# Feed-forward groups of 3, 4, 4 and 5 weight tiles, and conversion steps of two tiles interleaved

## The chip, the cores and the metric

The kernel runs on one core of a Trainium2 chip. The metric is the device time of one execution in microseconds, as the median of several runs. A profile is of one execution, and its times are counted from the start of its span. Engines are named as the profile names them: PE multiplies matrices, PEld is its weight load, DVE, ACT and POOL work on tiles element by element, SP issues transfers.

## The reference

Three parts follow one another; each takes the output of the one before.

```python
# attention over hashed buckets: 2 x 8 heads, 768 positions, 64 wide
mask = q_bucket[:, :, :, None] == k_bucket[:, :, None, :]
scores = np.where(mask, scale * q @ k.T, -1e9)
attn = exp(scores - scores.max(-1)); attn /= attn.sum(-1) + 1e-9
x = (attn @ v) laid out as 1536 tokens x 512
# first feed-forward part, w_in 512 x 2048, w_out 2048 x 512 (float64 in memory)
h = x @ w_in
x = where(h > 0, h, exp(min(h, 0)) - 1) @ w_out
# second part: 4 experts, each relu(x @ w1[e]) @ w2[e], weighted by normalized probabilities
```

## The kernel before

**Numbers.** Every matrix product is made of three PE products of two-part numbers (high part and rest), so each operand is split into a high and a low tile. The weights of the first feed-forward part are 64-bit in memory. [...]

**Weight tiles.** The hidden width 2048 is cut into 16 weight tiles of 128 columns of `w_in` and the matching 128 rows of `w_out`. A tile takes 18 steps, each taken from a list one at a time, most of them one instruction over half the tile (128x512): two on ACT (L243), then on DVE two each of L244, L245, L247, L249 and L250, then two additions L257 (on POOL, or on DVE if `adder` says so), one step that frees the raw buffer and lets SP issue the next load (`consumed`, L202), two splits (each ACT L274, then DVE L278; the first for the `w_in` half, the second for the `w_out` half), and one more that only keeps the books. There are three raw buffers, so a load goes out three tiles ahead.

**Groups.** Before the change there are four groups of four tiles. For each group the kernel goes through three blocks of 512 tokens, and for each block through the tiles of the group: 48 pairs (group, block, tile) in the list `seq` (L793). A pair has a first product l1 (L709 to L711, 12 matmuls) whose result goes through ACT L738 and L739, DVE L742, ACT L743 and POOL L747 to become `h`, and a second product l2 (L763, 12 matmuls) from `h`. After the last tile of a block the four PSUM tiles are added to the sum in SBUF (`epilogue`, L776: a copy by ACT L780 in the first group, DVE L782 after that).

**Order of the work.** The order is written out by hand, and each engine takes its instructions in the order in which they are issued. In step n of the main loop (L1203) the kernel issues l1 of pair n and its L738 and L739, then l2 of pair n-2 and its epilogue, then L742, L743 and L747 of pair n, and then some conversion steps (L837: nine a step in the first twelve steps, then six). Eight weight tiles have room in SBUF, and the dictionary `todo` (L795) says from which step on each is converted. The tiles are converted one after the other: all 18 steps of one, then those of the next.

**Ends of attention.** Three weight tiles (0, 1 and 2) are converted during attention (L674 to L681). The letters of `TAIL` (L75) order the last attention steps together with l1 of pairs 0 to 3 (`p`, `o`, `q`), l2 of pairs 0 to 2 (`k`), and conversion steps (`f`, 35 of them, with the additions on DVE; `s` runs what is missing of tile 3 and splits it). `c`, `n`, `g` finish the last attention output, which l1 needs for its last 128 input rows. In the ends of attention L747 is on DVE (`GL` is 0). Pair 1 uses a PSUM tile that l2 of pair 0 needs next.

Tiles are numbered t0 to t15 below, in the order of use.

Of the kernel before, what the change touches and what calls it, by code (L numbers as in the profile page):

```python
# [16 lines left out]
P = 128  # L17
# [18 lines left out]
def lsh_attention_moe_kernel(  # L36
# [14 lines left out]
    nc = tc.nc  # L51
# [3 lines left out]
    DFF = w_in.shape[1]  # L55
# [8 lines left out]
    TB = 512  # L64
    NTB = NT // TB
    GM = 8
    GP = 4
    G1 = DFF // (P * GP)
    NG = G1 + E
    NPRE = 2  # L70
    WA = 3
    ORDER = "CETHQtNLhlMmdV"
    WARM = (9, 2, 5)
    GL = 0.0
    TAIL = "AfffffffoqfpBpcpprffofffffpfpqppVfVfffVfncxkgfffgfozqfsfkffppffppoffqffk"  # L75

    mm = nc.tensor.matmul

# [104 lines left out]


    wide = w_in.dtype != F32
    wraw, w32, wt = {}, {}, {}

    raw_free, raw_used = [raw_p], []
    ld_n = [0]
    keep = {}  # L190
    ld_list = [(g, m) for g in range(NG) for m in range(0, GP if g < G1 else GM, 1 if wide and g < G1 else 2)]

    def loads():
        while ld_n[0] < len(ld_list) and raw_free:
# [7 lines left out]
    def consumed(g, m, split):  # L202
        if (not split) if wide and g < G1 else (split and m % 2):
            raw_free.append(raw_used.pop(0))
            loads()

    def load_w(g, m):
        if g < G1:
            a, b_, f0 = w_in, w_out, (g * GP + m) * P
        else:  # L210
            a, b_, f0 = w1[g - G1], w2[g - G1], m * P
        e = 1
        if wide and g < G1:
            a, b_, e = a.bitcast(I32), b_.bitcast(I32), 2
        n = 3 - e
        t = raw_free.pop(0).tile([P, 4 * DM], I32 if e == 2 else F32, tag="raw", name="raw")
        t1 = t[:, 0:2 * DM].rearrange("p (c f) -> p c f", c=NC)
        t2 = t[:, 2 * DM:4 * DM]
        nc.sync.dma_start(out=t1, in_=a[:, f0 * e:f0 * e + 2 * P].rearrange("(c p) f -> p c f", p=P))
        nc.sync.dma_start(out=t2.rearrange("p (m d) -> p m d", m=n),  # L220
                          in_=b_[f0:f0 + n * P, :].rearrange("(m p) d -> p m d", p=P))
        for i in range(n):
            wraw[g, m + i] = (t, t1, t2, i)
# [36 lines left out]
    def split_w(g, m, pool, eng, part=None):  # L260
        if part != 1:
            wt[g, m] = pool.tile([P, 4, DM], F32R, tag="w", name="w")
        t = wt[g, m]
        for i, s in enumerate(w32[g, m]):
            if part == 1 - i:
                continue
            hi, lo = t[:, 2 * i, :], t[:, 2 * i + 1, :]
            if i == 0:
                hi = hi.rearrange("p (c f) -> p c f", f=P)
                lo = lo.rearrange("p (c f) -> p c f", f=P)  # L270
            if "p" in eng:
                nc.gpsimd.tensor_scalar(out=hi, in0=s, scalar1=1.0, scalar2=1.0, op0=ALU.mult, op1=ALU.mult)
            else:
                nc.scalar.activation(out=hi, in_=s, func=ACTF.Copy)  # L274
            if "P" in eng:
                nc.gpsimd.tensor_tensor(out=lo, in0=s, in1=hi.bitcast(F32), op=ALU.subtract)
            else:
                nc.vector.tensor_tensor(out=lo, in0=s, in1=hi.bitcast(F32), op=ALU.subtract)  # L278
        if part != 0:
            del w32[g, m]  # L280
# [470 lines left out]
    def emit_l2(g, tb, ms):  # L751
        if ms[0] == 0:
            l2_t[g, tb] = [pools["ps2" if i < 2 else "ps3"].tile([P, 512], F32, tag=f"l2_{i}", name=f"l2_{i}")
                           for i in range(4)]
        parts = [(m, wt[g, m], *h_t.pop((g, tb, m))) for m in ms]
        for i in range(4):
            ps = l2_t[g, tb][i]
            r = slice(i * P, (i + 1) * P)
            for m, w, hh, hl in parts:
                w2h, w2l = w[:, 2, :], w[:, 3, :]  # L760
                ops = ((w2h[:, r], hh), (w2h[:, r], hl), (w2l[:, r], hh))
                for n, (a, b_) in enumerate(ops):
                    mm(ps, a, b_, start=(m == 0 and n == 0), stop=(m == GP - 1 and n == 2))  # L763
            if ms[-1] == GP - 1:
                epilogue(g, tb, i, ps)

    def acc_tile(tb):
# [20 lines left out]
    def wpool(m):  # L788
        return wa_p if m < NPRE else pools["wb" if m > NPRE else "wm"]

    LAG = 2
    due = []
    seq = [(g, tb, m) for g in range(G1) for tb in range(NTB) for m in range(GP)]  # L793

    todo = {GP * NTB * (g - 1) + max(3 * m, GP + 1 + m if g == 1 else 0): (g, m) for g in range(1, G1) for m in range(GP)}  # L795

    todo2 = {4: 0, 5: 1, 6: 2, 7: 3, 10: 4, 11: 5}
    conv = []

    def l1_step(n):  # L800
# [13 lines left out]
            f()  # L814
        del fill[:n]

    def slot_of(g, m):
        return wpool((g * GP + m) % GM)

    def l2_step(n, rest=None):  # L820
        if n < LAG:
            return
        rest = rest or []
        g, tb, m = seq[n - LAG]
        emit_l2(g, tb, range(m, m + 1))
        take(rest, 1)
        if g + 1 == G1 and tb * GP + m in todo2:
            prep2(todo2[tb * GP + m])
        due.extend([todo[n]] if n in todo else [])
        if due and not conv:  # L830
            g, m = due.pop(0)
            if (g, m) not in w32:
                conv.extend(conv_w(g, m, pools["w32"], 2))
                conv.append(lambda: consumed(g, m, False))
            conv.extend(lambda i=i: split_w(g, m, slot_of(g, m), "a", i) for i in range(2))
            conv.append(lambda: consumed(g, m, True))
        take(conv, 9 if n < GP * NTB else 6)  # L837

# [91 lines left out]
    def prep2(m):  # L932
        if m == 0:
            keep["cv"] = cv_p.tile([P, 2 * DM], F32, tag="w32", name="tmp")
            keep["tmp"] = keep["cv"][:, 0:DM].rearrange("p (k d) -> p k d", k=2)
            emit_pt()
        if m < 2:
            prep_w1(0, m)
        elif m < 6:
            prep_w2(0, m - 2)  # L940
# [166 lines left out]
            unit(v, a, hooks)  # L1107


    parts, outs, fill = [], [], []  # L1110
    at = {nm: 0 for nm in "VLkq"}
    at.update(s=NPRE + 1, f=NPRE + 1)

    def l1_start(m):
        ps, pa = l1_parts(*seq[m])
# [3 lines left out]
    def step(nm):  # L1119

        if nm in "AB":
            att_step(NU - 2 + "AB".index(nm))
        elif nm == "V":
            att_step(NU + at["V"])
        elif nm == "c":
            while done:
                emit_comb(done.pop())
        elif nm == "r":
            emit_rinv(NPAIR - 1)
            emit_rx(NPAIR - 1)  # L1130
        elif nm == "n":
            for half in range(2):
                ps = ps_t.tile([P, 512], F32, tag=f"pt{2 + half}", name="r")
                emit_norm(NPAIR - 1, half, ps)
                fin.append(lambda half=half, ps=ps: emit_fin(NPAIR - 1, half, ps[:, 0:HS]))
        elif nm == "g":
            fin.pop(0)()
        elif nm == "x":
            ps_late.close()
            open_pool("ps3", 1, None, PSUM)  # L1140
            open_pool("ring", 1, None, PSUM)
        elif nm == "z":
            late.close()
            open_pool("wb", GM - NPRE - 1)
            open_pool("near", 1)
            open_pool("accp", 1)
        elif nm == "p":
            if not parts:
                at["L"] += 1
                l1_start(at["L"])  # L1150
            take(parts, 1)
        elif nm == "o":
            m, ps = outs.pop(0)
            outq.extend(l1_out(*seq[m], ps, GL))
            take(outq, 1)
        elif nm == "q":
            take(outq, 1)
        elif nm == "k":
            l2_step(at["k"] + LAG)
        elif nm == "f":  # L1160
            if not fill:
                g, m = divmod(at["f"], GP)
                fill.extend(conv_w(g, m, pools["w32"], 2, nc.vector) + [lambda: consumed(g, m, False)])
                at["f"] += 1
            take(fill, 1)
        elif nm == "s":
            m = at["s"]
            while at["f"] <= m or at["f"] == m + 1 and fill:
                step("f")
            split_w(0, m, wpool(m), "a")  # L1170
            consumed(0, m, True)
        if nm in "Vks":
            at[nm] += 1

    fin, outq = [], []
# [19 lines left out]
    for nm in TAIL:  # L1195
        step(nm)
    assert not (parts or outs or outq or fin or done)
    conv.extend(fill)
    ahead = seq[GP:]
    ahead += [(G1 + gg, tb, m) for gg in range(2 * E) for tb in range(NTB) for m in range(4)]  # L1200
    for f in l1_step(GP):
        f()
    for n in range(GP + 1, len(seq) + LAG):  # L1203
        if ahead[0][0] == G1 and "hf" not in pools:
            open2()
        rest = l1_step(n)
        if n >= len(seq):
            l1_step(n)
        l2_step(n, rest)
# [32 lines left out]
```

## Time and profile before

| | |
|---|---|
| median of 3 runs | 1058.06 us |
| lowest and highest | 1055.71 and 1058.21 us |
| the profiled execution: its own time | 1054.75 us |
| its span | 1053.0 us |
| PE busy in the span | 1019.5 us (97%) |
| DVE, ACT, POOL busy | 826.4, 520.4, 499.3 us |
| attention, roughly | 0 to 262 us |
| first feed-forward part, main run | 262 to 546 us |
| second part | 546 to 1053 us |

PE counts as busy from a matmul's start to its modelled end, and neighbours overlap: the start-to-start distance says more than the busy time. A row of a timeline gives the start, the time, the engine, the line, the tile written and read, and in brackets how long the engine had been idle and what ended that.

### The profile page before, as it was taken

The page shows a single profiled execution, that of the slowest core. Times are in us where ns is not written, and L with a number is a line of the kernel's source. Part 1 is how long each engine was busy: PE and PEld are TensorE (multiplying, and loading weights), DVE is VectorE, ACT ScalarE, POOL GpSimd, SP SyncE. Part 2 cuts the span into 40 slices and gives each one's busy share as a digit, 9 for nine tenths or more (in the row PEclk, how much of TensorE's full clock was granted, in tenths as well). Part 3 has the DMA queues.
Part 4 walks back from the last instruction along what each step waited for, and adds up shares of the span by engine and source line. Part 5 has one row for each costly group of instructions (what it writes and reads, how often), then busy time and mean ns, then how long its engine had stood idle before and what let it go on. Part 6 is the DMA issues. An engine that isn't in the chain of part 4 may idle for free.

```text
span 1053.0 us, 16050 instructions
## 1 busy us (share of the span) xinstructions
PE 1019.5 (97%) x5886; PEld 890.4 (85%) x5886; DVE 826.4 (78%) x1295; ACT 520.4 (49%) x1024; POOL 499.3 (47%) x422
## 2 busy tenths in 40 slices
PE   8999999999899999998999999999999999999996
PEld 5898998888688887886788989898898989988896
DVE  6889889889656756673658778889898888989885
ACT  6898998897455443434533324233332333233322
POOL 3466776665225343432231243545555445464464
PEclk9999999999899999999999999999999999999999
DMA  7866676561212121210020020020200102010012
GB/s 182 156 143 147 144 173 144 126 185 41 80 41 80 41 81 40 80 41 1 21 90 2 1 99 13 1 81 5 96 11 26 56 11 91 11 66 16 2 50 71
DMA packets 72694, 72.24 MB, mean 69 GB/s; under 512 B 26132, under 2 KB 60648, under 8 KB 72616
## 3 DMA queue, kind: packets, MB, share of 16 engines
q1 hardware_dynamic: 72312, 71.14, 24.6%
q8 instruction: 47, 0.77, 0.3%
q14 instruction: 31, 0.25, 0.1%
q10 hardware_dynamic: 304, 0.07, 0.0%
HBM read 48.98 MB, written 3.21 MB: 50 GB/s over the span
## 4 chain that ended last, share of the span: by engine, by line
PE 34%; DVE 7%; POOL 6%; issue 5%; ACT 1%; POOLq 0%
PE l L1006 14%; POOL a L1022 4%; PE a L955 3%; PE a L954 3%; PE a L953 3%; PE l L763 2%; PE r L955 2%; PE r L954 2%; PE r L953 2%; DVE w L895 2%; DVE temps L982 1%; POOL hf L988 1%; POOL w L895 1%; DVE temps L984 1%; ACT op L891 1%
## 5 line engine op out<-in xcount | busy, mean ns | idle before, releaser
L1006 PEld LDWEIGHTS l<-w,op 128*128 128x128 f32 x2016 | 252.1, 188 | 13.6 <-ACT op L891 5.6
L1006 PE MATMUL l<-w,op 128*128 128x256 f32 x2016 | 255.7, 281 | 3.8 <-ACT op L891 3.8
L1022 POOL TENSOR_TENSOR a<-a,temps 128x512 f32<-128x512 f32 x84 | 124.3, 1502 | 60.1 <-DVE a L1017 60.1
L747 POOL TENSOR_TENSOR h<-g,h 128x512 fp32r<-128x512 f32 x44 | 62.9, 1430 | 170.5 <-ACT h L743 138.8
L763 PE MATMUL l<-h,w 128*128 128x512 f32 x576 | 140.4, 391 | 2.0 <-DVE g L742 1.5
L763 PEld LDWEIGHTS l<-h,w 128*128 128x128 f32 x576 | 107.7, 188 | 26.9 <-DVE g L742 2.0
L988 POOL TENSOR_TENSOR hf<-hf,temps 128x512 f32<-128x512 f32 x24 | 40.1, 1669 | 152.5 <-DVE op L895 143.7
L390 DVE TENSOR_SCALAR_CACHE_REDUCE mk<-s 128x768 f32<-128x768 f32 x96 | 91.3, 951 | 21.8 <-PE s L381 18.8
L423 DVE TENSOR_TENSOR ptl<-pt,pth 128x384 fp32r<-128x384 f32 x192 | 97.6, 549 | 11.0 <-ACT pth L426 11.0
L891 ACT ACTIVATE op<-temps 128x512 fp32r<-128x512 f32 x48 | 30.1, 627 | 153.8 <-DVE temps L984 153.8
L895 DVE TENSOR_TENSOR op<-hf,op 128x512 fp32r<-128x512 f32 x120 | 100.0, 849 | 4.4 <-ACT op L891 4.3
L891 ACT ACTIVATE op<-hf 128x512 fp32r<-128x512 f32 x120 | 74.1, 624 | 53.9 <-PE l L1006 29.9
L409 PE MATMUL pt<-cst,mk 128*128 128x128 f32 x576 | 94.8, 274 | 0.6 <-ACT mk L399 0.4
L399 ACT ACTIVATE mk<-mk,mn 128x768 f32<-128x768 f32 x96 | 89.7, 935 | 10.9 <-DVE mk L390 10.3
L426 ACT ACTIVATE pth<-pt 128x384 fp32r<-128x384 f32 x192 | 84.0, 482 | 8.2 <-PE pt L409 7.7
L380 PE MATMUL s<-ks,qs 128*128 128x512 f32 x192 | 80.2, 440 | 7.6 <-DVE mk L390 7.2
L409 PEld LDWEIGHTS pt<-cst,mk 128*128 128x128 f32 x576 | 71.0, 140 | 12.7 <-ACT mk L399 5.3
L955 PE MATMUL r<-xh,w 128*128 128x512 f32 x192 | 75.8, 395 | 0.0
L955 PE MATMUL a<-xh,w 128*128 128x512 f32 x192 | 75.6, 394 | 0.0
L954 PE MATMUL r<-xl,w 128*128 128x512 f32 x192 | 75.5, 393 | 0.0
L954 PE MATMUL a<-xl,w 128*128 128x512 f32 x192 | 75.4, 393 | 0.0
L953 PE MATMUL a<-xh,w 128*128 128x512 f32 x192 | 75.1, 391 | 0.0
(155 smaller groups left out, 2216.0 us busy)
## 6 DMA issues: line engine op xcount, KB each, us to landing
raw<-in_moe_w_dram SPq DMA_DIRECT2D x32, 512.0 KB
raw<-in_moe_w_in_dram SPq DMA_DIRECT2D x16, 512.0 KB
raw<-in_moe_w_out_dram SPq DMA_DIRECT2D x16, 512.0 KB
ks<-kh SPq DMA_DIRECT2D x15, 384.0 KB
qs<-qh SPq DMA_DIRECT2D x30, 192.0 KB
sk<-in_k_dram SPq DMA_DIRECT2D x8, 384.0 KB
sq<-in_q_dram SPq DMA_DIRECT2D x8, 384.0 KB
ks<-kl SPq DMA_DIRECT2D x16, 192.0 KB
```

What stands on the lines that cost most here:

```text
L390: nc.vector.tensor_scalar(out=e_t[u], in0=s_t.pop(u)[:, 0:S], scalar1=MASKED, scalar2=None, op0=ALU.min, op1=ALU.min, accum_out=mn)
L399: nc.scalar.activation(out=e, in_=e, func=ACTF.Exp, bias=mn_t.pop(u), scale=-1.0, accum_out=sums_t[g2][:, j, par:par + 1])
L409: nc.tensor.transpose(pt[:, i * P:(i + 1) * P], e_t[u][:, kb * P:(kb + 1) * P], ident)
L423: nc.vector.tensor_tensor(out=lo, in0=pt, in1=hi.bitcast(F32), op=ALU.subtract)
L763: mm(ps, a, b_, start=(m == 0 and n == 0), stop=(m == GP - 1 and n == 2))
L891: nc.scalar.activation(out=hi, in_=x, func=ACTF.Copy)
L895: e.tensor_tensor(out=lo, in0=x, in1=hi.bitcast(F32), op=ALU.subtract)
L953: mm(ps, wh[:, cs], xh[c][:, ts], start=(c == 0), stop=False)
L954: mm(ps, wh[:, cs], xl[c][:, ts], start=False, stop=False)
L955: mm(ps, wl[:, cs], xh[c][:, ts], start=False, stop=(c == NC - 1))
L1006: mm(ps[:, tt * HD:(tt + 1) * HD], a[:, cs], b_[:, k_], start=(n == 0), stop=(n == 11))
L1022: nc.gpsimd.tensor_tensor(out=x, in0=x, in1=keep[nm], op=ALU.add)
```

## The change

The groups get 3, 4, 4 and 5 tiles (`GS`), so that the first group needs only the three tiles converted during attention. `FT` lists the tiles in order. Tile 3 is now the first of the second group. In `TAIL` the `f` steps fall from 35 to 11, and none stands before the last attention steps are over; `s` is gone; all additions L257 go to POOL. The list of conversion steps is made by `new_conv`: the first six steps of a tile (L243, L244, L245) come first, then the splits of the tile before it, then the rest of this tile. `conv_step` runs the next one if its step number is reached. The main loop runs ten a step in steps 5 to 10 and seven from step 11 on. The preparation of the second part's first weights (`todo2`) is placed at other positions of the last group, which now has 15 pairs.

```diff
+    NPRE = 2
+    GS = (3, 4, 4, 5)
+    G1 = len(GS)
+    FT = [(g, m) for g in range(G1) for m in range(GS[g])]
-    TAIL = "AfffffffoqfpBpcpprffofffffpfpqppVfVfffVfncxkgfffgfozqfsfkffppffppoffqffk"
+    TAIL = "AoqpBpcpproppqppVVVncxkgogkqffzkffppppfffoffffq"
-                    mm(ps, a, b_, start=(m == 0 and n == 0), stop=(m == GP - 1 and n == 2))
-            if ms[-1] == GP - 1:
+                    mm(ps, a, b_, start=(m == 0 and n == 0), stop=(m == GS[g] - 1 and n == 2))
+            if ms[-1] == GS[g] - 1:
                 epilogue(g, tb, i, ps)
...
+    seq = [(g, tb, m) for g in range(G1) for tb in range(NTB) for m in range(GS[g])]
+
+    todo = [(seq.index((FT[t - GM][0], NTB - 1, FT[t - GM][1])) + LAG if t >= GM else 0, FT[t])
+            for t in range(GS[0], len(FT))]
+
+    todo2 = {5: 0, 6: 1, 8: 2, 10: 3, 12: 4, 13: 5}
...
+    def new_conv():
+
+        due, (g, m) = todo.pop(0)
+        steps = conv_w(g, m, pools["w32"], 2)
+        conv.extend((0, f) for f in steps[:6])
+        conv.extend(ends)
+        conv.extend((0, f) for f in steps[6:] + [lambda: consumed(g, m, False)])
+        ends[:] = [(due, lambda i=i: split_w(g, m, wpool(FT.index((g, m)) % GM), "a", i)) for i in range(2)]
+        ends.append((due, lambda: consumed(g, m, True)))
+        if not todo:
+            conv.extend(ends)
+
+    def conv_step(n):
+        if not conv and todo:
+            new_conv()
+        if conv and conv[0][0] <= n:
+            conv.pop(0)[1]()
...
-        take(conv, 9 if n < GP * NTB else 6)
+        for _ in range(0 if n <= GS[0] + 1 else 10 if n < NTB * GS[0] + LAG else 7):
+            conv_step(n)
...
         elif nm == "f":
-            if not fill:
-                g, m = divmod(at["f"], GP)
-                fill.extend(conv_w(g, m, pools["w32"], 2, nc.vector) + [lambda: consumed(g, m, False)])
-                at["f"] += 1
-            take(fill, 1)
-        elif nm == "s":
-            m = at["s"]
-            while at["f"] <= m or at["f"] == m + 1 and fill:
-                step("f")
-            split_w(0, m, wpool(m), "a")
-            consumed(0, m, True)
+            conv_step(0)
```

## Rows read from the trace of the kernel before

**Rows 1.** Three stretches: busy us and count per engine, granted clock, DMA share, GB/s.

```profile
270.00:280.00 10.00, 6.42 (x17) 4.65 (x18) 6.79 (x12) 3.05 (x6) 2.07 (x3) 0.66 0.17 49
...
400.00:410.00 10.00, 7.64 (x30) 5.55 (x29) 5.33 (x8) 3.07 (x6) 3.77 (x3) 0.92 0.14 40
...
470.00:480.00 10.00, 6.89 (x30) 5.08 (x28) 5.66 (x9) 2.83 (x5) 3.75 (x3) 1.00 0.00 0
```

**Rows 2.** Timeline, end of attention: start us, us, engine, line, tiles, [idle before].

```profile
262.12 0.95 PE L763 MATMUL l<-h,w 128*128 128x512 f32 x3
...
263.85 0.67 DVE L742 SCALAR_TENSOR_TENSOR g<-e,l 128x512 f32<-128x512 f32 x1
263.96 0.38 SPq L219 DMA_DIRECT2D raw<-in_moe_w_in_dram  x1
...
264.58 5.17 PE L763 MATMUL l<-h,w 128*128 128x512 f32 x21 [1.51 <-DVE g L742]
...
273.37 0.79 PE L709 MATMUL a<-xh,w 128*128 128x512 f32 x1 [3.62 <-ACT w L274]
...
284.52 0.39 PE L709 MATMUL r<-xh,w 128*128 128x512 f32 x1
```

**Rows 3.** Timeline around step 26 of the main loop, three engines.

```profile
399.20 0.39 PE L709 MATMUL a<-xh,w 128*128 128x512 f32 x1
...
402.19 0.67 DVE L742 SCALAR_TENSOR_TENSOR g<-e,r 128x512 f32<-128x512 f32 x1
...
404.85 2.52 POOL L257 TENSOR_TENSOR w<-w,raw 128x512 f32<-128x512 f32 x2
...
406.84 0.50 PE L709 MATMUL a<-xh,w 128*128 128x512 f32 x1 [1.96 <-ACT w L274]
...
414.69 0.39 PE L709 MATMUL r<-xh,w 128*128 128x512 f32 x1
```

**Rows 4.** Timeline of PE around step 38 of the main loop.

```profile
469.52 0.39 PE L709 MATMUL a<-xh,w 128*128 128x512 f32 x1
...
472.24 2.88 PE L763 MATMUL l<-h,w 128*128 128x512 f32 x12
477.84 0.50 PE L709 MATMUL a<-xh,w 128*128 128x512 f32 x1 [2.71 <-ACT w L274]
...
484.09 0.39 PE L709 MATMUL r<-xh,w 128*128 128x512 f32 x1
```

**Rows 5.** Groups by line, 290 to 560 us: busy us, mean ns, idle before, releaser.

```profile
L278 DVE TENSOR_TENSOR w<-w,w 128x512 fp32r<-128x512 f32 x24 | 22.7, 952 | 41.2 <-ACT w L274 40.1
L249 DVE TENSOR_SCALAR raw<-w 128x512 int32<-128x512 int32 x22 | 16.1, 767 | 0.0
L250 DVE SCALAR_TENSOR_TENSOR raw<-raw 128x512 f32<-128x512 uint32 x22 | 15.2, 730 | 0.0
L244 DVE TENSOR_SCALAR w<-w 128x512 f32<-128x512 f32 x20 | 14.6, 768 | 13.6 <-ACT w L243 13.6
...
L247 DVE SCALAR_TENSOR_TENSOR w<-raw,w 128x512 int32<-128x512 int32 x22 | 14.1, 680 | 0.0
...
L245 DVE TENSOR_SCALAR w<-w 128x512 int32<-128x512 int32 x20 | 7.5, 414 | 0.0
```

**Rows 6.** The same view for POOL: L257.

```profile
L257 POOL TENSOR_TENSOR w<-w,raw 128x512 f32<-128x512 f32 x20 | 25.6, 1304 | 0.0
```

**Rows 7.** Timeline of DVE and POOL, single rows from steps 5 to 25.

```profile
288.73 0.69 DVE L742 SCALAR_TENSOR_TENSOR g<-e,r 128x512 f32<-128x512 f32 x1 [2.03 <-ACT e L739]
...
290.88 0.76 DVE L249 TENSOR_SCALAR raw<-w 128x512 int32<-128x512 int32 x2
...
396.48 1.56 POOL L747 TENSOR_TENSOR h<-g,h 128x512 fp32r<-128x512 f32 x1 [2.68 <-issue]
...
396.81 1.86 DVE L249 TENSOR_SCALAR raw<-w 128x512 int32<-128x512 int32 x2
```

**Rows 8.** The page's line of GB/s in 40 slices.

```profile
GB/s 182 156 143 147 144 173 144 126 185 41 80 41 80 41 81 40 80 41 1 21 90 2 1 99 13 1 81 5 96 11 26 56 11 91 11 66 16 2 50 71
```

More of the change, by code (lines that the diff above doesn't have):

```diff
@@ L66, in lsh_attention_moe_kernel @@
     GM = 8
-    GP = 4
-    G1 = DFF // (P * GP)
+    NPRE = 2
+    GS = (3, 4, 4, 5)
+    G1 = len(GS)
+    FT = [(g, m) for g in range(G1) for m in range(GS[g])]
+    assert len(FT) == DFF // P and GS[0] == NPRE + 1
     NG = G1 + E
-    NPRE = 2
     WA = 3
@@ L185, in lsh_attention_moe_kernel @@
     wide = w_in.dtype != F32
+    assert wide
     wraw, w32, wt = {}, {}, {}
@@ L190, in lsh_attention_moe_kernel @@
     keep = {}
-    ld_list = [(g, m) for g in range(NG) for m in range(0, GP if g < G1 else GM, 1 if wide and g < G1 else 2)]
+    ld_list = [(g, m) for g in range(NG) for m in range(0, GS[g] if g < G1 else GM, 1 if g < G1 else 2)]
     def loads():
@@ L208, in load_w @@
         if g < G1:
-            a, b_, f0 = w_in, w_out, (g * GP + m) * P
+            a, b_, f0 = w_in, w_out, FT.index((g, m)) * P
         else:
@@ L791, in lsh_attention_moe_kernel @@
     LAG = 2
[L792 to L797, printed above, removed]
+    ends = []
+    seq = [(g, tb, m) for g in range(G1) for tb in range(NTB) for m in range(GS[g])]
+    todo = [(seq.index((FT[t - GM][0], NTB - 1, FT[t - GM][1])) + LAG if t >= GM else 0, FT[t])
+            for t in range(GS[0], len(FT))]
+    todo2 = {5: 0, 6: 1, 8: 2, 10: 3, 12: 4, 13: 5}
     conv = []
@@ L815, in take @@
         del fill[:n]
-    def slot_of(g, m):
-        return wpool((g * GP + m) % GM)
+    def new_conv():
[13 more added lines that the diff above has]
+            conv.pop(0)[1]()
     def l2_step(n, rest=None):
@@ L826, in l2_step @@
         take(rest, 1)
[L827 to L836, printed above, removed]
-        take(conv, 9 if n < GP * NTB else 6)
+        if g + 1 == G1 and tb * GS[g] + m in todo2:
+            prep2(todo2[tb * GS[g] + m])
+        for _ in range(0 if n <= GS[0] + 1 else 10 if n < NTB * GS[0] + LAG else 7):
+            conv_step(n)
     NGG = 2 * E
@@ L1107, in second @@
             unit(v, a, hooks)
-    parts, outs, fill = [], [], []
+    parts, outs = [], []
     at = {nm: 0 for nm in "VLkq"}
-    at.update(s=NPRE + 1, f=NPRE + 1)
     def l1_start(m):
@@ L1160, in step @@
         elif nm == "f":
-            if not fill:
-                g, m = divmod(at["f"], GP)
-                fill.extend(conv_w(g, m, pools["w32"], 2, nc.vector) + [lambda: consumed(g, m, False)])
-                at["f"] += 1
-            take(fill, 1)
-        elif nm == "s":
-            m = at["s"]
-            while at["f"] <= m or at["f"] == m + 1 and fill:
-                step("f")
-            split_w(0, m, wpool(m), "a")
-            consumed(0, m, True)
-        if nm in "Vks":
+            conv_step(0)
+        if nm in "Vk":
             at[nm] += 1
@@ L1197, in lsh_attention_moe_kernel @@
     assert not (parts or outs or outq or fin or done)
-    conv.extend(fill)
-    ahead = seq[GP:]
+    ahead = seq[GS[0] + 1:]
     ahead += [(G1 + gg, tb, m) for gg in range(2 * E) for tb in range(NTB) for m in range(4)]
-    for f in l1_step(GP):
+    for f in l1_step(GS[0] + 1):
         f()
-    for n in range(GP + 1, len(seq) + LAG):
+    for n in range(GS[0] + 2, len(seq) + LAG):
         if ahead[0][0] == G1 and "hf" not in pools:
```

## The prediction

> **What bounds the kernel now.** I read the stretches of ten microseconds first, to see where the PE does not work, then the timeline there, then the groups by line. From about 262 us on, PE does products back to back: an l1 or an l2 of twelve matmuls takes 2.72 us, so one step (l1 and l2) takes 5.44 us. That pace can be seen in step 38, where l1 starts at 469.52 and the next l2 at 472.24 us [rows 4]; two undisturbed steps are 10.88 us. The first part has few gaps, and three of them carry nearly all of the loss [rows 1]: one at the end of attention, with a granted clock of 0.66 in that stretch, one near 405 us (clock 0.92), and one near 475 us (clock 1.00). Their sizes, start to start:
>
> End of attention: from 262.12 to 284.52 us PE does three l2 and two l1, which need 5 x 2.72 = 13.6 us; it takes 22.40. The loss is 8.8 us [rows 2]. It has three parts: 1.51 us waiting for L742 of pair 1, which stood on DVE behind conversions until 263.85; 3.62 us waiting for ACT L274, the split of t3, and some tenths for its second half; and the rest, some 3.5 us, because PE ran at about half speed (the lower level, 1.2 of 2.4 GHz) after that pause.
>
> Step 26: from 399.20 to 414.69 us are 15.49 us for two steps, a loss of 4.6 us [rows 3]. The chain is L742 late at 402.19, POOL L257 of the same tile only behind it at 404.85, then the splits, and PE, waiting for them, at 406.84. After the pause it ran at the lower level for a while. Step 38: from 469.52 to 484.09 us are 14.57, a loss of 3.7 us, without a fall of the clock [rows 4]. Both are the same fault: in a list of one tile after the other, L257, L274 and L278 of a tile stand directly behind one another on three engines, and DVE stands still meanwhile. In the whole part DVE waited 40.1 us for L274 before L278 [rows 5].
>
> Together these gaps are 8.8 + 4.6 + 3.7 = **17.1 us**. The second part is a stream of products whose PE is busy throughout; the change does not touch it, so what is gained ahead of it should stay.
>
> **The change, part by part.** *No t3 needed in the first group, no conversion ahead of the last attention steps.* PE needs the same products up to l1 of pair 5 (three l2, two l1 from 262.12 on). L742 of pair 1 now follows the last attention work on DVE directly; its input is there by about 260 us, so the 1.51 us go. t3 is not waited for, so the 3.62 us go and with the pause the slow clock. What is late next here is the last attention output: l1 of pair 3 is now of the second token block and needs it, where before only pair 4 did. PV ends near 261.9 us; two ACT copies, one POOL addition, one DVE product and two POOL passes follow, some 5 us, so it is there near 267 us; that l1 starts at 262.12 + 3 x 2.72 = 270.3 us. h of pair 2 (L738, L739, L742, L743, L747 behind the same ACT copies) comes near 267.5 us for an l2 at 267.6: this could cost a few tenths. Gain 8.8, less 0.3.
>
> *Two tiles interleaved.* From step 12 on seven steps are run per pair, 18 per tile. A tile's POOL additions now lie nine to eleven places before its splits, so L278 no longer waits for L257 behind L747. Counting the list through: the splits of t7, t8, t9, t10 come in steps 14, 16, 19, 21 to 22, and are needed in steps 21 to 24; t11 to t15 come in steps 24 to 34 and are needed in steps 33 to 37. All have two steps (10.9 us) of room or more, so the gaps like those of steps 26 and 38 go: 4.6 + 3.7 us.
>
> *The new shortage: t3 to t6 in steps 5 to 11.* The first group now has nine pairs instead of twelve, and 24 of 35 conversion steps have left the attention's end, where they cost PE time but were done. Counting: 11 steps by the end of TAIL, ten in each of steps 5 to 10, seven in step 11. The splits of t3, t4, t5, t6 stand at places 22, 40, 58, 76 (counted from 1), that is, in steps 6, 7, 9 and 11; needed in steps 9, 10, 11 and 12. t6 has no step to spare. So DVE's lag decides. One tile takes on DVE 2 x (0.768 + 0.414 + 0.680 + 0.767 + 0.730 + 0.952) = 8.6 us by the mean times [rows 5]; where its two L249 run as fast as they did once, 0.76 us for both [rows 7], it takes 8.6 - (1.53 - 0.76) = 7.8 us. Ten steps of 18 are 4.3 to 4.8 us. With 0.6 us for L742 and, where a step's list begins with L243 or a split, a wait behind L742, L743 and L243 (13.6 us for ten pairs of L244 [rows 5], 1.3 to 1.4 us each), that is 4.9 to 6.8 us per step of 5.44.
>
> On time, L742 starts 4.2 us after its l1 (284.52 to 288.73 [rows 2, 7]). I follow DVE through the list at 7.8 us per tile, the start of L742 counted from the start of l1 of its step: step 5 at 4.2; step 6 at 4.2 (waits 1.3, then L278, L247, L249, L250); step 7 at 6.3; step 8 at 6.6; step 9 at 5.7; step 10 at 6.6; step 11 at 5.1. In step 11, two L244 and two L245 of t7 come first, then L278 of t6, which ends at 8.7 us. PE wants t6's high half at 5.4 and its low half at 5.9 us, so PE waits 2.8 us. At 8.6 us per tile the lag grows and the wait is 4.6 us. A pause of this size cost a fall of the clock once (step 26, some 2 us on top) and once not (step 38). So 2.8 to 7 us; I take **4.5**, near the middle, since neither tile time nor clock is settled by a row.
>
> POOL's rule: the two L249 took 0.76 us at 290.88, while POOL was idle, and 1.86 us at 396.81, with POOL's L747 running beside them [rows 7]. This speaks against the change: interleaving puts the additions of one tile beside the steps of the other, and all additions are now on POOL, 1.3 us each [rows 6]. The Trainium skill says as much (SBUF — State Buffer, Who interferes with whom): DVE and GpSimd have one pair of SBUF ports in common, held by one instruction at a time, and an instruction of the other engine that needs it is blocked until the end. The trace agrees with it in these two rows. If all of these pairs took the longer time, a tile would cost some 10 us by the longest rows; that is the third case below.
>
> *Loads.* A load goes out when a tile's additions are done. t6's left at 263.96 us [rows 2]; now t3's additions run on POOL in step 5, so it leaves near 285 us. It is 1 MB; at the page's best slice of 185 GB/s [rows 8] that is 5.7 us, at half that rate 11.4 us. Its first use is in step 9, near 304 us. Cover 8 us or more, nothing taken. Nothing but loads stands in SP's queue in these steps. *Epilogues, products, the second part's preparation* keep their number (four epilogues per block and group, 48 pairs); the preparation moves one or two steps ahead, and its buffers (tiles t8 to t13) are free by then. Taken as nothing, 0.5 us either way.
>
> **Sum.** 8.5 + 4.6 + 3.7 - 4.5 = 12.3 us saved. The profiled execution took 1054.75 us, which is 3.3 us under the median; from it, 1042.4. The median of 1058.06 less 12.3 is 1045.8; I forecast **1045.5**.
>
> **The rivals.** *DVE keeps up* (waits under 2.8 us in step 12): for it, DVE's own idle time is large in the trace of before, and ACT and POOL have room; against it, t6's splits stand behind four instructions of t7. It gives 14 to 16.6 us, 1041.5 to 1044. *POOL contention, faster still than before:* at about 9.3 us per tile DVE falls one microsecond behind in each of steps 6 to 11, t5 is waited for too, and the clock falls: 7 to 13 us of new waits, 3.5 to 9.6 us saved, 1048.5 to 1054.5.
>
> *Slower than before:* the same place, steps 9 to 12, but every tile of the second group late. At 10 us per tile (the longest rows) ten steps take 5.6 us, with L742 and the wait 7.5, which is 2.1 us too many in each of six steps: 12.6 us of lag, 2.8 us for the order of t6, and three pauses with a fall of the clock of 2 to 2.4 us each, some 22 us. That is 1063 us. It decides from 17 us of new waits on, and needs POOL beside nearly every DVE instruction; POOL works only some 4 us of each 5.4 us step in this case (L747 1.4 us and on average 1.1 additions of 1.3 us make 2.9), so it is unlikely. *It doesn't do what it says:* the end of attention was limited by its own chain, and the 8.8 us become waits for the last output; then about 3.5 us are left, which the noise of the measurement nearly hides: 1054.5.
>
> **How the numbers follow.** Forecast (new wait of 2.8 to 7 us) 0.52; DVE keeps up 0.20; contention 0.15; attention's own chain or other waits that eat the gain 0.08; slower 0.05. What a measurement of this kernel can tell from no change is about 0.3%, 3.2 us: faster takes the first three, all but a tenth of the third, and a little of the fourth, 0.87; same 0.08; slower 0.05. The range of 8 in 10 takes in the first two cases and most of the third: low, 17 us saved from the median and a little for a run like the profiled one, 1039.5; high, 1053.
>
> **What would show it.** Right: between the start of the first l2 and l1 of pair 5 about 13.6 us and no clock below the upper level; no wait of PE for L274 or L278 after step 13; the idle time of L278 behind L274 down from 41 us to well under half; one wait of PE for t6's splits near the twelfth l1 of the main run, of 2.8 to 4.6 us. Wrong: PE waiting for the second token block's input at pair 3; waits for L274 in steps 10 or 11 too; the second part longer than 507 us; h (L747) late for l2 because DVE lags by two steps.

## The result and the profile after

The kernel after takes **1047.49 us** (median of 4 runs, 1045.87 to 1048.54) against 1058.13 us (1055.71 to 1060.03) of the kernel before in the same comparison: ratio **0.9899**, 95% interval 0.9875 to 0.9923. The forecast was 1045.5 us, range 1039.5 to 1053. The profiled execution of after took 1047.5 us, its span is 1045.7 us.

Line numbers of after in this part of the kernel are those of before plus 3: L763, L709, L742, L747, L257, L274, L278, L244, L245 of before are L766, L712, L745, L750, L260, L277, L281, L247, L248 of after.

The stretches of ten microseconds of after, columns as in [rows 1] (the first line names them):

```profile
core 0: us, PE busy (x) PEld busy (x) DVE busy (x) ACT busy (x) POOL busy (x), PEclk, DMA share, GB/s
270.00:280.00 10.00, 10.00 (x45) 8.20 (x44) 5.16 (x12) 5.49 (x9) 0.00 (x0) 1.00 0.00 0
...
310.00:320.00 10.00, 7.61 (x33) 5.61 (x31) 9.42 (x14) 7.47 (x14) 6.18 (x4) 1.00 0.34 105
320.00:330.00 10.00, 7.33 (x24) 5.58 (x23) 4.67 (x7) 2.23 (x4) 1.76 (x2) 0.66 0.30 105
...
400.00:410.00 10.00, 10.00 (x46) 8.20 (x45) 7.59 (x13) 3.84 (x7) 6.64 (x4) 1.00 0.25 79
470.00:480.00 10.00, 10.00 (x46) 8.29 (x45) 3.56 (x6) 3.97 (x7) 1.29 (x1) 1.00 0.00 0
```

The three gaps of [rows 1] are gone: PE is busy for the whole ten microseconds at 270, 400 and 470, with a granted clock of 1.00. One new gap stands between 310 and 330 us, and behind it the clock is at 0.66. All waits of PE for another engine between 250 and 560 us (total us, times, longest us):

```profile
PE r L714 <- DVE w L281: 2.7, 1, 2.7
PE r L712 <- ACT w L277: 2.0, 1, 2.0
PE a L714 <- DVE w L281: 0.3, 1, 0.3
```

The timeline of PE shows where they are (start us, us, engine, line, tiles, idle before):

```profile
264.49 8.57 PE L766 MATMUL l<-h,w 128*128 128x512 f32 x36
...
278.37 0.39 PE L712 MATMUL r<-xh,w 128*128 128x512 f32 x1
...
308.55 2.96 PE L766 MATMUL l<-h,w 128*128 128x512 f32 x12
...
312.31 0.50 PE L714 MATMUL a<-xh,w 128*128 128x512 f32 x1 [0.35 <-DVE w L281]
...
314.70 2.88 PE L766 MATMUL l<-h,w 128*128 128x512 f32 x12
...
319.63 0.50 PE L712 MATMUL r<-xh,w 128*128 128x512 f32 x1 [2.05 <-ACT w L277]
...
323.04 0.80 PE L714 MATMUL r<-xh,w 128*128 128x512 f32 x1 [2.67 <-DVE w L281]
...
327.42 2.92 PE L766 MATMUL l<-h,w 128*128 128x512 f32 x12
```

From the first l2 at 264.49 to l1 of pair 5 at 278.37 are 13.88 us, where [rows 2] had 22.40. In step 12 the two splits of t6 are late. From the l2 of step 11 at 314.70 to that of step 12 at 327.42 are 12.72 us instead of 5.44: 7.3 us lost, 4.7 of them waiting, the other 2.6 with the clock down. Step 11, with the small wait, took 6.15 us (308.55 to 314.70), 0.7 too many. Together that is 8.0 us.

To compare kernels without the attention, whose code is unchanged and whose first l2 started 2.4 us later in this execution (1.4 of them are a longer wait for its first load, 2.3 us in place of 0.9), I use the **main run**: from the first l2 (L766) to the first product of the second part (L1018 of after, L1006 of before). It is 286.30 us in before (262.12 to 548.42) and 276.99 us in after (264.49 to 541.48), 9.3 us less. The terms: 8.5 (end of attention) + 8.3 (the gaps of steps 26 and 38) - 8.0 (steps 11 and 12) = 8.8, and 0.5 stays without a name. The second part is equal, 504.6 and 504.2 us to the end of the span.

**Why the splits are late**: POOL, ACT and DVE of after around step 12.

```profile
314.85 2.83 POOL L750 TENSOR_TENSOR h<-g,h 128x512 fp32r<-128x512 f32 x1 [3.82 <-issue]
317.64 2.71 POOL L260 TENSOR_TENSOR w<-w,raw 128x512 f32<-128x512 f32 x2
```
```profile
318.95 0.63 ACT L277 ACTIVATE w<-w 128x512 fp32r<-128x512 f32 x1 [0.48 <-POOL w L260]
```
```profile
317.72 2.92 DVE L247 TENSOR_SCALAR w<-w 128x512 f32<-128x512 f32 x2
320.56 1.82 DVE L248 TENSOR_SCALAR w<-w 128x512 int32<-128x512 int32 x2
322.30 1.28 DVE L281 TENSOR_TENSOR w<-w,w 128x512 fp32r<-128x512 f32 x2
```

The first wait, for L277 of t6, hangs on POOL: L277 follows L260, and L260 stood until 317.64 behind an L750 that took 2.83 us (1.29 undisturbed, the one at 281.29). The second wait hangs on DVE: L281 of t6 stands there behind a pair of L247 and a pair of L248 of t7. The pair of L247 begins with POOL's two L260 of t6 and ends with them, 2.92 us; the pair of L248 lies beside the next L750 and takes 1.82 us. The groups by line, 290 to 560 us as in [rows 5] (the view is the same):

```profile
L260 POOL TENSOR_TENSOR w<-w,raw 128x512 f32<-128x512 f32 x24 | 33.8, 1426 | 6.3 <-DVE raw L253 6.3
...
L247 DVE TENSOR_SCALAR w<-w 128x512 f32<-128x512 f32 x22 | 23.1, 1082 | 10.0 <-ACT w L246 10.0
L281 DVE TENSOR_TENSOR w<-w,w 128x512 fp32r<-128x512 f32 x26 | 21.5, 858 | 9.8 <-ACT w L277 9.8
L248 DVE TENSOR_SCALAR w<-w 128x512 int32<-128x512 int32 x22 | 15.5, 738 | 0.0
L250 DVE SCALAR_TENSOR_TENSOR w<-raw,w 128x512 int32<-128x512 int32 x24 | 15.5, 679 | 0.0
...
L253 DVE SCALAR_TENSOR_TENSOR raw<-raw 128x512 f32<-128x512 uint32 x24 | 15.5, 679 | 0.0
...
L252 DVE TENSOR_SCALAR raw<-w 128x512 int32<-128x512 int32 x24 | 12.5, 552 | 0.0
```

Against [rows 5] DVE's wait behind L277 fell from 40.1 to 9.8 us, as the interleaving should make it. But L247 rose from 768 to 1082 ns, L248 from 414 to 738, and POOL's L260 from 1304 [rows 6] to 1426. L252, L253 and L281 became faster, by 0.05 to 0.2 us.

### The profile page after: what moved, and what is told of

It is laid out like the page before. It is cut to its first block, busy times and chain, and to the rows that moved or that the text cites. A ratio compares the mean times of both kernels' runs of the same rounds, so it can differ in the third digit from the quotient of the medians.

```text
span 1045.7 us, 16064 instructions
## 1 busy us (share of the span) xinstructions
PE 1016.3 (97%) x5886; PEld 889.8 (85%) x5886; DVE 831.8 (80%) x1289; ACT 521.1 (50%) x1024; POOL 513.1 (49%) x428
## 4 chain that ended last, share of the span: by engine, by line
PE 32%; issue 10%; POOL 7%; DVE 7%; ACT 1%; POOLq 0%
PE l L1018 15%; POOL a L1034 4%; PE a L967 3%; PE a L966 3%; PE a L965 3%; PE r L967 2%; PE r L966 2%; PE r L965 2%; DVE w L907 2%; DVE temps L994 1%; POOL h L750 1%; POOL hf L1000 1%; PE l L766 1%; POOL w L907 1%; DVE temps L996 1%
## 5 line engine op out<-in xcount | busy, mean ns | idle before, releaser
L1018 PEld LDWEIGHTS l<-w,op 128*128 128x128 f32 x2016 | 252.1, 188 | 13.3 <-ACT op L903 5.2
L1018 PE MATMUL l<-w,op 128*128 128x256 f32 x2016 | 255.5, 281 | 3.8 <-ACT op L903 3.8
L766 PE MATMUL l<-h,w 128*128 128x512 f32 x576 | 139.8, 391 | 0.1
L750 POOL TENSOR_TENSOR h<-g,h 128x512 fp32r<-128x512 f32 x44 | 66.7, 1516 | 143.2 <-ACT h L746 93.9
L766 PEld LDWEIGHTS l<-h,w 128*128 128x128 f32 x576 | 107.9, 188 | 24.5 <-POOL h L750 0.9
L1000 POOL TENSOR_TENSOR hf<-hf,temps 128x512 f32<-128x512 f32 x24 | 40.1, 1670 | 155.7 <-DVE op L907 146.9
```

Source lines behind the costliest of these rows:

```text
L766: mm(ps, a, b_, start=(m == 0 and n == 0), stop=(m == GS[g] - 1 and n == 2))
L1018: mm(ps[:, tt * HD:(tt + 1) * HD], a[:, cs], b_[:, k_], start=(n == 0), stop=(n == 11))
```

## The experiments

No experiment changes what is computed. Each ratio is against runs of before taken beside it (medians 1056.75 to 1058.13 us). Main run, waits and clock are of one profiled execution of each kernel. Waits are those of PE in step 12 (for L277, for L281); the clock is that of 320 to 330 us.

| kernel | median us | ratio (95%) | main run us | waits | clock |
|---|---|---|---|---|---|
| before | 1058.13 | 1 | 286.30 | other places | |
| one_after_other | 1051.97 | 0.9938 (0.9913 to 0.9962) | 283.02 | 3.84, 0 | 0.83 |
| interleaving_alone | 1048.18 | 0.9914 (0.9887 to 0.9941) | 278.13 | 0, 0 | 1.00 |
| after | 1047.49 | 0.9899 (0.9875 to 0.9923) | 276.99 | 2.05, 2.67 | 0.66 |
| pool_left_out_early | 1045.88 | 0.9886 (0.9872 to 0.9899) | 276.28 | 2.82, 1.35 | 0.66 |
| splits_sooner | 1045.41 | 0.9889 (0.9873 to 0.9906) | 274.69 | 3.07, 0.40 | 0.83 |
| late_and_sooner | 1043.99 | 0.9872 (0.9851 to 0.9892) | 274.81 | 1.97, 0.58 | 0.83 |
| seven_more_late | 1043.64 | 0.9865 (0.9841 to 0.9889) | 274.38 | 1.36, 1.78 | 0.83 |
| early_and_sooner | 1043.30 | 0.9878 (0.9858 to 0.9897) | 273.30 | 0.71, 0.60 | 1.00 |
| seven_more_early | 1043.72 | 0.9862 (0.9834 to 0.9890) | 272.51 | 1.12, 1.78 | 1.00 |
| additions_on_dve | 1041.92 | 0.9860 (0.9846 to 0.9874) | 271.94 | 0.66, 1.66 | 1.00 |
| dve_adds_and_early | 1041.18 | 0.9846 (0.9829 to 0.9863) | 270.70 | 0, 0.91 | 1.00 |
| dve_adds_and_late | 1040.71 | 0.9847 (0.9831 to 0.9864) | 270.62 | 0, 0.91 | 1.00 |

**The change without the interleaving, and the interleaving without the groups.** First the new groups, the new order at the end of attention and the new steps per pair, with tiles one after the other:

```
-        conv.extend((0, f) for f in steps[:6])
-        conv.extend(ends)
-        conv.extend((0, f) for f in steps[6:] + [lambda: consumed(g, m, False)])
+        conv.extend((0, f) for f in steps + [lambda: consumed(g, m, False)])
...
-        if not todo:
-            conv.extend(ends)
+        conv.extend(ends)
```

> The changed kernel without the interleaving: all 18 steps of a tile, then those of the next; groups, order at the end of attention and steps per pair as changed. Theory A (interleaving removes the gaps at the start of the last two groups): they come back, 8.3 us for both, and DVE's idle time before L278 behind L274 rises from 9.8 us to some 40: about 1055 us. Rival B (the gaps go because seven steps per pair leave two or more pairs of room): no wait of PE for L274 or L278 after step 13, idle time before L278 some 30 to 40 us all the same, and only the wait in step 12 differs (t6's splits end at place 72 in place of 77, but directly behind its additions, so 5 to 10 us against 7.3): 1046 to 1050 us.

Its waits of PE between 255 and 560 us:

```profile
PE l L766 <- DVE a L785: 3.9, 3, 3.1
PE r L712 <- ACT w L277: 3.8, 1, 3.8
PE a L714 <- DVE w L281: 0.4, 1, 0.4
PE l L766 <- ACT a L783: 0.3, 1, 0.3
```

No wait for a split after step 12, as theory B said, yet the time lies between the two theories. DVE still waits 37.6 us for L277 here, and the lag comes out at another place: an l2 at 455.36 us waits 3.1 us for the epilogue's L785 on DVE, which stands behind an L281 that waited 1.85 us for L277, and the clock from 450 to 460 us is 0.84. From the l2 at 446.55 to that at 462.51 us 5.1 us are lost. Then the groups and the end of attention of before with interleaved tiles. This kernel differs from before in a second thing: a tile's steps start as soon as the list has room, where before held each tile back for its place in `todo`.

```
+            steps = conv_w(g, m, pools["w32"], 2)
+            conv.extend((0, f) for f in steps[:6])
+            conv.extend(ends)
+            conv.extend((0, f) for f in steps[6:] + [lambda: consumed(g, m, False)])
+            del ends[:]
+        ends.extend((due, lambda i=i: split_w(g, m, slot_of(g, m), "a", i)) for i in range(2))
```

> The kernel before with groups of four and its own order at the end of attention, but with the steps of two tiles interleaved and no conversion held back for its place in time (six steps per pair as before, nine in the first twelve). Both theories: the loss at the end of attention (8.8 us) stays, and the gaps near steps 26 and 38 (4.6 and 3.7 us) go, so about 1050 us (8.3 us less than before). If the change's gain came from the end of attention alone, it stays at 1058.

Its waits of PE between 255 and 560 us, with the line numbers of before:

```profile
PE a L709 <- ACT w L274: 3.6, 1, 3.6
PE l L763 <- DVE g L742: 1.5, 1, 1.5
PE l L763 <- POOL h L747: 0.5, 1, 0.5
PE a L711 <- DVE w L278: 0.2, 1, 0.2
```

The main run is 8.2 us shorter than before's, where the forecast had 8.3 for this part. The waits left are those of the end of attention, with the sizes of [rows 2], and 0.5 us for L747 at 518.82 us, which before has too (526.73). But this does not show that the interleaving closed the two gaps. The splits of t11, which PE waited for in the gap of step 26, start as follows in before and in this kernel:

```profile
406.16 0.63 ACT L274 ACTIVATE w<-w 128x512 fp32r<-128x512 f32 x1 [2.64 <-POOL w L257]
```
```profile
383.54 1.14 ACT L274 ACTIVATE w<-w 128x512 fp32r<-128x512 f32 x2
```

They come 22.6 us earlier, those of t15 28.9 us (477.15 and 448.22), at the same number of steps a pair. So they are ready well ahead of their use, and in one_after_other, where no tile is held back for its place either, no split is waited for after step 12 without any interleaving. Tiles that are ready ahead of their use are enough to close these gaps; interleaving with before's starts was not tried. What the interleaving is worth by itself is seen between one_after_other and after, which differ in nothing else: 6.0 us of main run (283.02 and 276.99), 5.1 of them around the l2 at 455.36 us, which in after does not wait for a DVE that stood still. Over before, the groups without interleaving save 3.3 us, interleaving with the earlier start 8.2, the change 9.3: the groups win 8.5 us at the end of attention and give most of it back in steps 11 and 12.

**Is it where the conversion stands, or how long it takes?** Seven more conversion steps before the main loop, once behind attention's end and once ahead of it:

```
-    TAIL = "AoqpBp...fffoffffq"
+    TAIL = "AoqpBp...fffoffffqfffffff"
```

> The changed kernel with seven more conversion steps at the end of the written order, behind the last attention work, where DVE stood idle for 3.5 us. t6's splits move from step 11 to step 10. Theory (the place of t6's splits in the list is what is short): the wait in step 12, 7.3 us with the slow clock behind it, goes to under 1 us: 1040 to 1042 us. Rival (POOL's contention with DVE slows the whole conversion, so that the lag only shows elsewhere): 3 us or more of waits in steps 9 to 12 remain: 1043 to 1047 us.

```
-    TAIL = "AoqpBp...
+    TAIL = "AfffffffoqpBp...
```

> The changed kernel with seven conversion steps put back ahead of the last two attention steps, where the kernel before had them. t6's splits move to step 10 as well, so the wait in step 12 should go (7 us). Theory (the loss at the end of attention came from the need for t3, and from DVE work there only in part): DVE has some 4 us of added work, of which PE sees 1 to 2 us: 1041 to 1043 us. Rival (conversions ahead of the last attention steps are what cost the time): 1.5 us of wait for L742 of pair 1, and a late end of attention, 4 us or more: 1045 us or more.

PE in step 12 of the late kernel, then its clock:

```profile
316.57 0.50 PE L712 MATMUL r<-xh,w 128*128 128x512 f32 x1 [1.36 <-ACT w L277]
...
319.08 0.50 PE L714 MATMUL r<-xh,w 128*128 128x512 f32 x1 [1.78 <-DVE w L281]
```
```profile
320.00:330.00 10.00, 10.00 (x39) 8.09 (x38) 7.13 (x11) 4.82 (x8) 7.41 (x4) 0.83 0.06 18
```

The same of the early kernel:

```profile
316.29 0.50 PE L712 MATMUL r<-xh,w 128*128 128x512 f32 x1 [1.12 <-ACT w L277]
...
318.81 0.50 PE L714 MATMUL r<-xh,w 128*128 128x512 f32 x1 [1.78 <-DVE w L281]
```
```profile
320.00:330.00 10.00, 10.00 (x46) 8.28 (x45) 8.32 (x12) 5.57 (x10) 7.63 (x5) 1.00 0.05 10
```

Seven steps, more than a third of a tile's eighteen, took only 1.6 to 1.8 us off the waits. The early kernel has no wait of PE at attention's end, so seven conversion steps there cost PE nothing as long as none of them is waited for. This points to the need for t3, and not the place of the conversion, as what cost most of the 8.8 us in before; whether all 24 steps could have stayed was not tried. The two main runs differ by 1.9 us; their waits differ by 0.24 us, and one has a slow stretch behind it. Their medians do not differ, so a difference of this size between two main runs can be that of single executions.

**The order of the splits.** Ahead of the next tile's L247 and L248 instead of behind them:

```
-        conv.extend((0, f) for f in steps[:6])
+        conv.extend((0, f) for f in steps[:2])
         conv.extend(ends)
-        conv.extend((0, f) for f in steps[6:] + ...
+        conv.extend((0, f) for f in steps[2:] + ...
```

> The kernel after, with the splits of a tile (L277, L281) run behind the two L246 of the next tile, and not behind its two L247 and two L248 as well. In the kernel after, DVE spent 317.72 to 322.30 us on these four instructions (2.92 and 1.82 us beside POOL's L260) before it ran L281 of t6, for which PE waited. Theory A (the four instructions that stand ahead of L281 make the second pause): PE's wait for L277 in step 12 stays at some 2 us, since L277 hangs on L260 alone; the wait for L281 falls from 2.7 us to under 0.6; the slow stretch shrinks or goes. Main run (first l2 to the second part's first row) 276.99 less 2.2 to 4.5 us, so 272.5 to 274.8; time 1043 to 1045.3. Theory B (DVE is short of time as such, the order only says where it shows): L281 now holds DVE up behind L277, its idle time for L277 rises from 9.8 us to over 25, and new waits of PE in steps 12 to 40 take the gain back: main run 276 to 279.

PE, DVE and the group of L281 in this kernel:

```profile
319.97 0.50 PE L712 MATMUL r<-xh,w 128*128 128x512 f32 x1 [3.07 <-ACT w L277]
...
321.10 0.80 PE L714 MATMUL r<-xh,w 128*128 128x512 f32 x1 [0.40 <-DVE w L281]
```
```profile
319.95 2.78 DVE L281 TENSOR_TENSOR w<-w,w 128x512 fp32r<-128x512 f32 x2 [1.80 <-ACT w L277]
322.66 0.75 DVE L247 TENSOR_SCALAR w<-w 128x512 f32<-128x512 f32 x2
```
```profile
L281 DVE TENSOR_TENSOR w<-w,w 128x512 fp32r<-128x512 f32 x26 | 27.1, 1056 | 36.7 <-ACT w L277 36.1
```

The second wait went as theory A said, and the main run of 274.69 is inside its range. But the first wait did not stay at 2 us, it rose to 3.07. DVE's idle time behind L277 came back, as theory B said, 36.1 us, though it made no new wait of PE. L247 is at 0.75 us for a pair now and L281 is the stretched one, 2.78 us for two beside POOL. The order decides which of DVE's instructions meets POOL, not whether one does. Together with the seven steps it gave nothing:

> Both the seven conversion steps more at the end of the attention's list and the splits directly behind the two L246 of the next tile. Seven more alone left waits of PE of 1.36 us for L277 and 1.78 us for L281 and a clock of 0.83 behind them (main run 274.38). If the order ahead of L281 makes the second of these waits: L281's goes to under 0.5 us, the clock stays up or nearly, main run 271 to 272.7, time 1040.5 to 1043. If DVE is short as such: main run 274 or more.

> The seven conversion steps ahead of the end of attention, and the splits directly behind the two L246 of the next tile. Seven more early alone left waits of 1.12 us for L277 and 1.78 us for L281 without a fall of the clock (main run 272.51). Order theory: the wait for L281 goes to under 0.5 us, main run 270.7 to 271.5, that is within 1.5 us of products back to back, time 1040 to 1043; what is left is L277's 1.1 us. If DVE is short as such, or the attention's end now pays for the seven steps: 272.5 or more.

In both the wait for L281 is only 0.6 us, but an l2 near 298 us now waits 0.73 us for the epilogue's L783 on ACT (in the early kernel another, at 361 us, 0.66 us for L785), and the main runs, 274.81 and 273.30, are no shorter than with the seven steps alone. The order theory's figures were missed by about 2 us.

**Take POOL away.** First the additions of t3 to t6 on DVE (`conv_w` makes a weight tile's 32-bit numbers out of its 64-bit ones):

```
-        steps = conv_w(g, m, pools["w32"], 2)
+        steps = conv_w(g, m, pools["w32"], 2, nc.vector if g == 1 else nc.gpsimd)
```

> The kernel after, with the two additions of each of t3 to t6 (L260) on DVE and not on POOL, 0.68 us each there, so that 1.36 us of work per tile move to DVE. Contention theory (an instruction of POOL on the same memory ports stretches DVE's pair of L247 from 0.75 to 2.3 to 2.9 us and that of L248 to 1.86): without L260 on POOL in steps 5 to 11 the pairs fall back to 0.75 to 1.5 us, which is worth more than the 1.36; the waits of PE in step 12 fall from 4.7 us to under 2, no slow clock, main run 276.99 less 3 to 7.5 us, 269.5 to 274. Rival (DVE is short of work time alone, the stretch in the records is only waiting that would be there anyway): DVE gets 1.36 us per tile more, 5.4 us over four tiles, and the waits in steps 11 and 12 grow to 6 us or more, main run 278 to 284.

```profile
317.25 0.50 PE L712 MATMUL r<-xh,w 128*128 128x512 f32 x1 [0.66 <-ACT w L277]
...
319.64 0.50 PE L714 MATMUL r<-xh,w 128*128 128x512 f32 x1 [1.66 <-DVE w L281]
```

DVE got 1.3 us more work per tile and was earlier. The waits fell from 4.7 to 2.3 us (under 2 expected), the clock stayed up, and the main run is 5.05 us shorter. Two things can have done this: the pairs of L247 are shorter (0.75 to 1.41 us for the first three), and L260 no longer stands behind L750 on POOL, so that L277 comes sooner. This run does not separate them. The remaining stretch lies beside L750, and L750 is stretched as well:

```profile
312.51 4.06 POOL L750 TENSOR_TENSOR h<-g,h 128x512 fp32r<-128x512 f32 x1 [4.47 <-ACT h L746]
```
```profile
315.92 2.39 DVE L247 TENSOR_SCALAR w<-w 128x512 f32<-128x512 f32 x2
```

Then L750 of steps 5 to 11 on DVE as well, so that POOL has nothing to do there:

```
-        first, *rest = l1_out(*x, l1_mm(*x))
+        first, *rest = l1_out(*x, l1_mm(*x), 0.0 if n <= 11 else 1.0)
```

> The additions of t3 to t6 on DVE, and in steps 5 to 11 h's low part as well (L750), so that POOL has nothing in these steps. Ports theory: with POOL idle every pair of L247 takes 0.75 us and every pair of L248 0.75 us, none over 0.9, until the step where POOL starts again; a tile then takes about 7.4 us on DVE. But each step has L750 and a wait for ACT's L746 on DVE, 0.70 us and some 0.8 us, which is 1.5 us per step against the 1.6 us or less that the stretched pair cost: the waits in step 12 come out between 1 and 6 us, main run 271 to 277, no better than with the additions alone. Rival (the stretch of L247 does not come from POOL but from something else in these steps, such as reads of the same tile by ACT or DMAs that write SBUF): pairs of L247 of 1.4 us and more are still there with POOL idle.

Two of its pairs of L247, one of its L750 on DVE, and the first instruction of POOL after 269.7 us:

```profile
308.22 0.95 DVE L247 TENSOR_SCALAR w<-w 128x512 f32<-128x512 f32 x2
...
319.07 0.69 DVE L750 TENSOR_TENSOR h<-g,h 128x512 fp32r<-128x512 f32 x1 [0.70 <-ACT h L746]
319.68 0.76 DVE L247 TENSOR_SCALAR w<-w 128x512 f32<-128x512 f32 x2
```
```profile
329.15 1.60 POOL L750 TENSOR_TENSOR h<-g,h 128x512 fp32r<-128x512 f32 x1 [59.45 <-ACT h L746]
```

With POOL idle from 269.70 to 329.15 us all four pairs in that time take 0.76 us (once 0.95, which stays unexplained), where they took 2.3 to 2.9. That settles what stretches them; it does not make the stretch the whole cause of PE's waits. The waits are back at 2.82 and 1.35 us all the same, as expected: each step now holds 0.69 us of L750 and 0.70 us of waiting for ACT's L746 on DVE. So here moving work off POOL paid only where it brought no wait of DVE with it.

**The best version** joins the additions on DVE with the seven steps.

> The additions of t3 to t6 on DVE, and seven conversion steps more at the end of the attention's list, so that the splits of t6 come in step 10 and not 11. Additions alone left two waits of PE in step 12, 0.66 us for L277 and 1.66 us for L281, main run 271.94, 1041.9 us. If those waits are DVE's remaining lag: seven steps are some 3.5 us of DVE, more than the 2.3 us that are missing, so both go to under 0.5 us together; main run 269.3 to 270.2 (products back to back: 286.30 less the 17.1 us of gaps is 269.2); time 1038.5 to 1041. Rival (the late steps delay what comes behind them, as they did with the splits sooner: an epilogue's ACT copy or h late for an l2): a wait of 0.5 us or more at another place, main run 271 or more.

> The additions of t3 to t6 on DVE, and the seven conversion steps ahead of attention's end. Lag theory: no wait of PE over 0.5 us in the main run, 269.3 to 270.2; time 1038.5 to 1041. Rival (seven steps ahead of attention's end cost the attention or its last output): main run still short, but the first l2 stands later and the time is 1041.9 or more.

```profile
317.88 0.50 PE L714 MATMUL r<-xh,w 128*128 128x512 f32 x1 [0.91 <-DVE w L281]
```

This is the late kernel's only wait of PE in the main run; the early kernel has the same, 0.91 us. Both main runs (270.62 and 270.70 us) are 1.4 to 1.5 us from products back to back, a little more than expected, because 0.9 us of wait stayed. The early kernel's first l2 does not stand later than the late one's (263.23 and 263.68 us), so nothing speaks for its rival. Their ratios, 0.9847 and 0.9846, lie below after's with no overlap of the intervals. Which of the two is better cannot be told, nor whether the seven steps add anything to the time of additions_on_dve (0.9846 to 0.9874).

## Why the prediction was right, and where it was off

- **What bounds the kernel, the three gaps**: right. All three went, and nothing else became late in the rest of the first part.
- **End of attention, 8.5 us**: right, 22.40 to 13.88 us. Neither the second token block's input at pair 3 nor h of pair 2 was waited for. The rival *attention's own chain* falls with this. None of the three parts of the loss comes back in seven_more_early, with seven of the 24 conversion steps put back.
- **The gaps of steps 26 and 38, 8.3 us**: the amount is right, its reason is not shown. The prediction gave two, the additions that lie further ahead of the splits and the two steps of room or more. No PE wait for L277 or L281 came after step 12 in after, and none in one_after_other either, so room is enough without interleaving. That DVE waits less behind L277 (9.8 us against 37.6) is the interleaving's doing, and on top of the groups it is worth 6.0 us.
- **The new wait in step 12, 4.5 us**: place and tile (t6) right, **the size is the term that failed**: 7.3 us in step 12 and 0.7 in step 11, 8.0 in all, beyond the term's own range of 2.8 to 7. The waiting itself, 4.7 us, is what the prediction had at its slower tile time, 4.6; of the 3.5 us that 4.5 fell short, 2.6 are the fall of the clock, left half in and half out, and 0.7 step 11. The 4.6 came out partly by luck: DVE's tile was taken at 7.8 to 8.6 us and is 2 x (1.082 + 0.738 + 0.679 + 0.552 + 0.679 + 0.858) = 9.2 us by the means of after, and the prediction followed DVE alone, where 2.05 of the 4.7 us are for L277, behind POOL.
- **POOL's rule**: the row pair 0.76 and 1.86 us [rows 7] was read rightly (POOL's next instruction there starts at 291.44 us, 0.2 us before the shorter pair ends), and then given to a rival with a chance of 0.15, because POOL works only part of a step (4 us of 5.4 by the text, 2.9 by its own sum; in after 6.18 of the ten us from 310). That argument failed: where L260 is released by DVE's L253, DVE goes on to L247 of the next tile, and for all four tiles up to step 12 the pair of L247 (284.59, 297.63, 307.56 and 317.72 us) lay beside POOL's additions. POOL's share of the step says nothing when the program itself puts the two side by side. The Trainium skill (SBUF — State Buffer, Who interferes with whom) has the pair of ports that DVE and GpSimd have in common locked by one of the two engines at a time. The traces agree: 2.92 us beside L260, 0.76 us with POOL idle.
- **The rival "contention"**: its mechanism is the one that the runs show (new waits of 7 to 13 us; 8.0 measured); its time, from 1048.5 on, was not reached. The forecast's own account holds for the rest. So the result lies at the border of the two.
- **"DVE keeps up" and "slower"**: fallen; t5 cost 0.35 us of waiting, and no other tile of the second group was late.
- **Loads, epilogues, second part**: right. No wait of PE, DVE or ACT for a load in the main run; the second part is equal within 0.4 us.
- **Sum**: forecast 12.3 us saved, 9.3 measured in the main runs of the two profiled executions, 10.6 in the medians. The whole difference to the forecast of the main run, 3.0 us, is the new wait's 3.5 less the 0.5 that stays without a name. That the time came within 2 us of 1045.5 is in part luck: the medians moved 1.3 us further than the main runs, and no row shows why.

## What to carry to other kernels

When two chains are interleaved over several engines, look up which instructions of one will now lie beside which of the other and cost them at the time that they take together, from a row that shows the pair; the average share of an engine does not bound that. A wait that a regrouping creates can cost more than the waiting, 2.6 us of slow clock on 4.7 us of waits here, so it should be taken at its upper end. A gap before a late tile may close by starting the tile earlier as well as by reordering its steps; a kernel that does both does not tell which it was. And a dependence may be removed without moving the work: here seven of the conversion steps ahead of attention's end were free once nothing waited for them.

## What the runs showed of the hardware

- A pair of DVE tensor_scalar passes (L247, 128x512 f32) took 0.75 us alone and 2.3 to 2.9 us beside POOL's tensor_tensor; DVE's L281 with two inputs, 1.28 us for two, took 2.78 beside it (splits_sooner).
- It goes the other way too, and further than expected: POOL's L750, 1.29 us undisturbed, took 4.06 us in additions_on_dve, where DVE ran L253, L260 and L745 without a break from 312.92 us on, none of them longer than elsewhere in the trace. By the records, which are rough for POOL, POOL was held up over several DVE instructions and not over one.
- Nearly the same pauses of PE, 1.36 and 1.78 us in one kernel and 1.12 and 1.78 us in another, were followed by a granted clock of 0.83 (partly the lower level, 1.2 of 2.4 GHz) in the one and 1.00 in the other; their main runs differ by 1.9 us.
